# Counting channel work from the issue of a crossbar transpose, and writing the last output half in two pieces

One core of one Trainium2 chip (the other cores idle). The metric is the device time of one execution in microseconds; the time of a kernel is the median of its runs.

## The reference

Attention with squared ReLU, then an MLP mixer over tokens and channels: 8 batches, 12 heads, 448 tokens, head size 64, so 768 channels.

```python
scores = q @ k.T / sqrt(64);  attn = relu(scores)**2 / 448
x = (attn @ v), heads side by side                 # [8, 448, 768]
u = x + (relu(x.T @ w_tok1) @ w_tok2).T            # token product, 448 -> 256 -> 448
out = u + relu(u @ w_ch1) @ w_ch2                  # channel product, 768 -> 1536 -> 768
```

## The kernel before

Attention goes by "fours" of heads, 24 in all, in a loop of rounds. Round `i` makes the scores of four `i`, the values and the token products of four `i - 1`. The channel products of earlier batches lie in a queue as units (`channel1`: six matmuls of 448 columns; `channel2`: twelve of 384 columns, an add, and a store after each second one), and `fill` draws from it between the pieces of attention, so that TensorE always has something to do. The token product needs `x` with tokens on the partitions; from four 8 on that turn is a crossbar transpose by DMA (`x_back`), and what `fill` puts between the issue of the transpose and `token1_main` is what hides it.

```python
    def x_back(i, place="bank", copy=None):
        ...
        if i >= XDMA:                                   # XDMA = 8; round i + 1 issues it
            nc.sync.dma_start_transpose(
                out=x_sb.rearrange("n r c d -> n (r c) d"),
                in_=xT[b % 2][:, 2 * d : 2 * d + 2, :].rearrange("n r t -> n (r t)"),
            )
            return
        ...                                             # earlier: eight TensorE transposes and a copy

    def token1_main(i):
        ...                                             # six matmuls L294 that read x_sb

    C1 = 6 * 189
    C2 = 12 * 163

    def fill(share, least=0):
        if not queue:
            return
        credit[0] += share * rate[0]
        done = 0
        while queue and (credit[0] > 0 or done < least):
            cost, unit = queue.pop(0)
            credit[0] -= cost
            unit()
            done += 1

    for i in range(DB + 1, ND + 2):                     # rounds 4 to 25
        ...                                             # scores 0 and 1, values(i - 1), values_out, scores 2
        if i - 1 < XDMA:
            fill(1 / 3, least=1)
        if 0 <= i - 1 < ND:
            x_back(i - 1)                               # the issue
        ...                                             # u_back: transposes of u on the same queue; loads
        if i - 1 >= XDMA:
            fill(0.37, least=1)                         # "the first fill"
        ...                                             # scores 3 and 4, transposes of q and k
        if slow:                                        # rounds up to 6
            token1(i - 1)
            fill(1 / 3, least=1)
        else:
            fill(0.37, least=1)                         # "the second fill"
            if back:
                token1_main(i - 1)
        ...
```

In `channel2` the last half of the last tile is one block of 384 columns: twelve matmuls, one add, and two stores of 64 rows, one from SyncE's queue and one from ScalarE's.

## Time and profile before

| | before |
|---|---|
| median of its runs | 378.77 us (378.59 to 379.48, 4 runs; the prediction knew three of them) |
| span of the profiled execution | 375.9 us |
| TensorE busy | 364.3 us (97%) |
| TensorE's wait for a transpose (L294) | 1.0 us, one time |
| last matmul to the end | 4.2 us |

The busy share says only who the bound is. What a change of order can win is in the idle time of that engine, place by place; the lines are in the prediction below. A wait in the timeline stands in brackets after the row that waited: its length in us and what ended it.

### The profile page before, as it was taken

How to read it: one execution, taken by the hardware profiler on the slowest of the kernel's cores; microseconds unless marked ns; L12 is line 12 of the kernel's file. 1: busy time of each engine (PE TensorE's matmuls, PEld its weight loads, DVE VectorE, ACT ScalarE, POOL GpSimd, SP SyncE). 2: the span in 40 equal slices, each digit the busy share in tenths (PEclk: the TensorE clock that was granted, in tenths of full speed). 3: DMA queues.
4: the chain of work that ended last, by engine and by line, in shares of the span. 5: the costliest groups of instructions: out<-in, count | busy, mean ns of one | idle time of the engine just before them, and what ended most of it. 6: DMA issues, size and time to landing. Idle time of an engine off the chain costs nothing.

```text
span 375.9 us, 10212 instructions
## 1 busy us (share of the span) xinstructions
PE 364.3 (97%) x4367; PEld 200.6 (53%) x4367; DVE 212.8 (57%) x412; ACT 211.6 (56%) x313; POOL 100.7 (27%) x187
## 2 busy tenths in 40 slices
PE   7889999999999989999999999999999999999995
PEld 3544555555555545565555655555555654555563
DVE  2996688766568456475654685375555755131021
ACT  4987888776544357725775457752775456412400
POOL 8975448303130322330330304312210000000000
PEclk9999999999999999999999999999999999999999
DMA  8999999923999867656755577847550424233023
GB/s 152 122 148 201 172 206 178 179 44 68 138 158 213 169 101 115 89 99 158 99 96 91 112 146 132 129 58 158 111 94 13 103 76 99 56 70 85 0 64 105
DMA packets 69405, 43.32 MB, mean 115 GB/s; under 512 B 43440, under 2 KB 65904, under 8 KB 69360
## 3 DMA queue, kind: packets, MB, share of 16 engines
q0 software_dynamic: 24496, 21.49, 40.0%
q1 hardware_dynamic: 44560, 20.75, 25.6%
q8 instruction: 34, 0.56, 0.6%
q10 hardware_dynamic: 304, 0.43, 0.4%
q14 instruction: 11, 0.09, 0.1%
HBM read 43.42 MB, written 11.01 MB: 145 GB/s over the span
## 4 chain that ended last, share of the span: by engine, by line
PE 87%; DVE 6%; ACT 3%; DMA 2%; issue 1%; SPq 0%; ACTq 0%; DVEq 0%
PE m_ps L425 29%; PE m_ps L386 28%; PE acc_ps L205 9%; PE sc_ps L172 8%; PE h_ps L335 4%; PE t_ps L294 3%; PE qkT_ps L148 3%; DVE at L193 2%; ACT at L186 2%; DMA x_sb<-xT 1%; DVE uT_sb L345 1%; PE t_ps L310 1%; DMA k_first<-in_k_dram 1%; PE t_ps L276 1%; DVE qkT L162 1%; PE x_ps L258 1%
## 5 line engine op out<-in xcount | busy, mean ns | idle before, releaser
L186 ACT ACTIVATE at<-sc_ps 128x896 bf16<-128x896 f32 x167 | 144.9, 924 | 50.0 <-PE sc_ps L172 50.0
L193 DVE TENSOR_TENSOR at<-at 128x896 bf16<-128x896 bf16 x168 | 99.0, 625 | 52.2 <-ACT at L186 52.0
L386 PE MATMUL m_ps<-uT_sb,wc 128*128 128x448 bf16 x564 | 115.4, 353 | 0.2 <-DVE uT_sb L345 0.2
L425 PE MATMUL m_ps<-wc,r_sb 128*128 128x384 bf16 x672 | 115.3, 326 | 0.0
L425 PEld LDWEIGHTS <-r_sb 128*128 128x128 bf16 x672 | 63.8, 98 | 47.7 <-issue 6.4
L393 ACT ACTIVATE r_sb<-m_ps 128x448 bf16<-128x448 f32 x94 | 51.3, 546 | 56.4 <-PE m_ps L386 56.0
L386 PEld LDWEIGHTS <-wc 128*128 128x128 bf16 x564 | 52.4, 98 | 53.2 <-issue 7.9
L432 DVE TENSOR_TENSOR out_sb<-m_ps,u_sb 128x384 f32<-128x384 f32 x56 | 31.0, 553 | 48.3 <-PE m_ps L425 47.6
L172 PE MATMUL sc_ps<-qkT 64*64 64x448 bf16 x672 | 54.1, 358 | 1.0 <-ACT at L186 0.6
L205 PE MATMUL acc_ps<-at,v_raw 64*64 64x448 bf16 x672 | 41.0, 351 | 0.9 <-ACT x_sb L267 0.5
L223 DVE TENSOR_SCALAR xT<-acc_ps 128x448 bf16<-128x448 f32 x45 | 26.1, 619 | 27.6 <-PE acc_ps L205 27.6
L608 POOL COPY gate<-x_sb 1x1 bf16<-1x1 bf16 x12 | 2.7, 221 | 127.9 <-DMA x_sb<-xT 127.9
L84 POOL DMA_DIRECT2D q_raw<-in_q_dram x48 | 29.0, 616 | 19.6 <-DMA wc<-in_moe_w_ch_dram 16.7
L345 DVE TENSOR_TENSOR uT_sb<-h_ps,xT 128x448 bf16<-128x448 f32 x48 | 27.7, 615 | 10.5 <-PE h_ps L335 10.4
L84 POOL DMA_DIRECT2D v_raw<-in_v_dram x48 | 29.6, 645 | 6.0 <-DMA wc<-in_moe_w_ch_dram 4.4
L162 DVE COPY qkT<-qkT_ps 128x896 bf16<-128x896 bf16 x45 | 25.9, 615 | 9.2 <-PE qkT_ps L148 9.2
L320 ACT ACTIVATE r_sb<-t_ps 128x256 bf16<-128x256 f32 x36 | 11.8, 381 | 31.7 <-PE t_ps L310 27.6
L205 PEld LDWEIGHTS <-v_raw 64*64 64x64 bf16 x672 | 21.8, 106 | 14.6 <-issue 4.9
L172 PEld LDWEIGHTS <-qkT 64*64 64x64 bf16 x672 | 17.5, 105 | 21.6 <-issue 17.7
L84 POOL DMA_DIRECT2D k_raw<-in_k_dram x46 | 28.2, 637 | 1.7 <-issue 1.7
L335 PE MATMUL h_ps<-wt,r_sb 128*128 128x448 bf16 x96 | 22.3, 353 | 0.0
L294 PE MATMUL t_ps<-x_sb,wt 128*128 128x256 bf16 x108 | 14.7, 273 | 1.0 <-DMA x_sb<-xT 1.0
(50 smaller groups left out, 146.6 us busy)
## 6 DMA issues: line engine op xcount, KB each, us to landing
out_dram<-out_sb SPq DMA_DIRECT2D x54, 192.0 KB, 2.8
q_raw<-in_q_dram POOLq DMA_DIRECT2D x48, 112.0 KB, 4.2
v_raw<-in_v_dram POOLq DMA_DIRECT2D x48, 112.0 KB, 5.0
k_raw<-in_k_dram POOLq DMA_DIRECT2D x46, 112.0 KB, 4.8
wc<-in_moe_w_ch_dram POOLq DMA_DIRECT2D x4, 1152.0 KB, 10.6
u_sb<-uT_sb SPq DMA_TRANSPOSE x48, 2.6
x_sb<-xT SPq DMA_TRANSPOSE x16, 3.3
k_first<-in_k_dram SPq DMA_DIRECT2D x1, 224.0 KB, 3.7
```

The lines of the kernel that those rows point to most:

```text
L84: eng.dma_start(out=dst[64 * r : 64 * (r + 1)].rearrange("p g c d -> p g (c d)"), in_=src[b, h0 : h0 + 2].rearrange("g (p c) d -> p g (c d ...
L162: (nc.scalar.copy if split and r == 0 else nc.vector.tensor_copy)(sb[:, r].rearrange("n w t -> n (w t)"), parts[r][:, : 2 * S])
L172: nc.tensor.matmul(ps[64 * r : 64 * (r + 1), g, :S], lhsT=sb[h, r, 1, c * 64 : (c + 1) * 64], rhs=sb[h, r, 0, :], start=True, stop=True, s ...
L186: nc.scalar.activation(at, ps[:, :, :S], AF.Relu)
L193: nc.vector.tensor_tensor(out=at, in0=at, in1=at, op=ALU.mult)
L205: nc.tensor.matmul(ps[r][64 * g : 64 * (g + 1), :S], lhsT=v_raw[h, g, c, :], rhs=at[h, g, :], start=(c == 0), stop=(c == QC - 1), skip_gro ...
L335: nc.tensor.matmul(parts[r][:, :S], lhsT=r1[:, j, r * 128 : (r + 1) * 128], rhs=wt2[:, j, :], start=(j == 0), stop=(j == JC - 1),)
L345: nc.vector.tensor_tensor(out=uT_tiles[b // 2][:, 2 * d + r, off : off + S], in0=parts[r][:, :S], in1=xT[b % 2][:, 2 * d + r, :S], op=ALU.add,
L386: nc.tensor.matmul(ps[:, :S], lhsT=wc1[:, g, e * 128 : (e + 1) * 128], rhs=uT[:, g, off : off + S], start=(g == 0), stop=(g == CC - 1),)
L393: nc.scalar.activation(r2[:, e, off : off + S], ps[:, :S], AF.Relu)
L425: nc.tensor.matmul(ps[:, :HN], lhsT=r2[:, e, t * 128 : (t + 1) * 128], rhs=wc2[:, e, cols], start=(e == 0), stop=(e == EC - 1),)
L432: nc.vector.tensor_tensor(out=o[:, cols].rearrange("n (g d) -> n g d", d=128), in0=ps[:, :HN].rearrange("n (g d) -> n g d", d=128), in1=u_ ...
```

## The change

Its intent: the `credit` of `fill` is an average over rounds, so a round whose units happen to be small can leave too little work behind the transpose. The new floor `upto` counts what was emitted since the issue and goes on drawing until 4400 ns' worth stands ahead of `token1_main` (the costs `C1` and `C2` are in ns: matmuls of 448 columns start 189 ns apart in the trace, those of 384 columns 163 ns). The second part cuts the last output half into 256 and 128 columns, so that the add and the store that come after the last matmul are smaller.

```diff
--- before.py
+++ after.py
@@ -447,6 +447,33 @@
         if half == 1:
             out_tiles.pop((b, t))
 
+    def channel2_last(b, t):
+
+        r2, o = r2_tiles[b // 2], out_tiles[b, t]
+        cuts = (HN, HN + 256, DM)
+        for lo, hi in zip(cuts, cuts[1:]):
+            ps = ps_mm.tile([128, 512], FP32, tag="bank", name="m2_ps")
+            for e in range(EC):
+                nc.tensor.matmul(
+                    ps[:, : hi - lo],
+                    lhsT=r2[:, e, t * 128 : (t + 1) * 128],
+                    rhs=wc2[:, e, lo:hi],
+                    start=(e == 0),
+                    stop=(e == EC - 1),
+                )
+            nc.vector.tensor_tensor(
+                out=o[:, lo:hi].rearrange("n (g d) -> n g d", d=128),
+                in0=ps[:, : hi - lo].rearrange("n (g d) -> n g d", d=128),
+                in1=u_tiles[b][:, lo // 128 : hi // 128, t - chunks(b).start, :],
+                op=ALU.add,
+            )
+            for k in range(2):
+                n, c = divmod(2 * t + k, QC)
+                rows = out[2 * (b // 2) + n].rearrange("(p c) m -> c p m", c=QC)
+                (nc.scalar if k else nc.sync).dma_start(
+                    out=rows[c, :, lo:hi], in_=o[64 * k : 64 * (k + 1), lo:hi]
+                )
+
     queue, later = [], []
     C1 = 6 * 189
     C2 = 12 * 163
@@ -456,7 +483,10 @@
             queue.append((C1, lambda e=e: channel1(b, e)))
         for t in chunks(b):
             for j in range(2):
-                later.append((C2, lambda t=t, j=j: channel2(b, t, j)))
+                last = b == B - 1 and t == NT - 1 and j == 1
+                unit = channel2_last if last else channel2
+                args = (b, t) if last else (b, t, j)
+                later.append((C2, lambda unit=unit, args=args: unit(*args)))
         if b > 0:
             queue.extend(later)
             later.clear()
@@ -466,14 +496,17 @@
     credit = [0.0]
     rate = [EC * C1 / 3.5]
 
-    def fill(share, least=0):
+    since = [0.0]
+
+    def fill(share, least=0, upto=0):
         if not queue:
             return
         credit[0] += share * rate[0]
         done = 0
-        while queue and (credit[0] > 0 or done < least):
+        while queue and (credit[0] > 0 or done < least or since[0] < upto):
             cost, unit = queue.pop(0)
             credit[0] -= cost
+            since[0] += cost
             unit()
             done += 1
 
@@ -598,6 +631,7 @@
             fill(1 / 3, least=1)
         if 0 <= i - 1 < ND:
             x_back(i - 1)
+        since[0] = 0.0
         if i > 2 * DB + 1:
             if i == 2 * DB + 2:
                 hold_back(1, x_tiles[i - 1][:1, 0, 0, :1])
@@ -623,7 +657,7 @@
             token1(i - 1)
             fill(1 / 3, least=1)
         else:
-            fill(0.37, least=1)
+            fill(0.37, least=1, upto=4400 if back else 0)
             if back:
                 token1_main(i - 1)
         if i < ND:
```

## The prediction

> **What bounds the kernel now.** I read the page's busy line and slices first, then the list of who waited for whom (TensorE alone), then the timeline around the one wait that the change aims at, and last the end of the timeline.
>
> ```profile
> PE 364.3 (97%) x4367; PEld 200.6 (53%) x4367; DVE 212.8 (57%) x412; ACT 211.6 (56%) x313; POOL 100.7 (27%) x187
> PE   7889999999999989999999999999999999999995
> PEclk9999999999999999999999999999999999999999
> ```
>
> TensorE is the bound: 364.3 of 375.9 us, at full clock. So 11.6 us are all that can be won without taking work off TensorE. The windows of 10 us put them: 6.0 us in the first 40 us, 4.2 us after the last matmul, 1.0 us between 130 and 140 us, 0.2 to 0.3 us in two other windows. The list of TensorE's waits says what the middle one is:
>
> ```profile
> PE warm_ps L488 <- DVE warm L484: 1.2, 1, 1.2
> PE t_ps L294 <- DMA x_sb<-xT: 1.0, 1, 1.0
> PE qkT_ps L148 <- ACT k_raw L89: 0.9, 1, 0.9
> ```
>
> The columns are the total, how often, and the longest, in us. One single token product (L294) of 16 fed by a crossbar transpose waited for it, 1.0 us. The other long waits are of the start. Here is that place, round 11 of the main loop:
>
> ```profile
> 132.91 0.34 DVE L232 TENSOR_SCALAR xT<-acc_ps 128x64 bf16<-128x64 f32 x2
> 133.39 1.23 SPq L249 DMA_TRANSPOSE x_sb<-xT  x1
> 134.96 2.44 PE L386 MATMUL m_ps<-uT_sb,wc 128*128 128x448 bf16 x12
> 138.40 0.55 PEld L294 LDWEIGHTS <-wt 128*128 128x128 bf16 x6 [1.45 <-DMA x_sb<-xT]
> 138.41 0.83 PE L294 MATMUL t_ps<-x_sb,wt 128*128 128x256 bf16 x6 [1.01 <-DMA x_sb<-xT]
> ```
>
> The transpose is issued at 133.39; TensorE is through with its filler (two channel1 units) at 137.40 and then stands to 138.41. So its **lead** (issue to the earliest start of the token product) is 4.01 us and the landing took about 5.0. Round 14, where nothing waits, is the comparison that I lean on most:
>
> ```profile
> 178.56 1.25 SPq L249 DMA_TRANSPOSE x_sb<-xT  x1
> 179.31 3.58 PE L386 MATMUL m_ps<-uT_sb,wc 128*128 128x448 bf16 x18
> 182.59 0.18 POOL L608 COPY gate<-x_sb 1x1 bf16<-1x1 bf16 x1 [13.89 <-DMA x_sb<-xT]
> 182.73 0.82 PE L294 MATMUL t_ps<-x_sb,wt 128*128 128x256 bf16 x6
> ```
>
> Lead 182.73 - 178.56 = 4.17 us, and the gate copy shows the landing just before 182.59 (the trace has 182.47, 3.9 us after issue): 0.25 us to spare. The page's median landing is 3.3 us, so there must be a reason for 5.0.
>
> ```profile
> q8 instruction: 34, 0.56, 0.6%
> ```
>
> 34 packets of 16,384 bytes are instruction fetches. 0.56 MB over 2 x 4367 TensorE instructions is 64 bytes each, so I take this queue to be TensorE's. In the packet records one starts at 136.32 and takes 0.92 us, and from 136.4 on single 256-byte transposed rows take up to 1.57 us where they usually take 0.02. I put all the landings beside the fetches: with one starting 2.5 to 2.9 us after the issue the transpose took 5.4, about 5.0 and 4.7 us (issues at 103.14, 133.39, 207.09); 0.9 us after it, 3.9 us; just before, well before or well after it, 3.0 to 3.3 us, but for one of 4.05 (issue at 118.31) that fetches don't explain. So the 1.0 us is a short lead meeting a late fetch.
>
> The end:
>
> ```profile
> 363.74 7.96 PE L425 MATMUL m_ps<-wc,r_sb 128*128 128x384 bf16 x48
> 370.38 2.45 ACTq L444 DMA_DIRECT2D out_dram<-out_sb  x2
> 371.74 0.56 DVE L432 TENSOR_TENSOR out_sb<-m_ps,u_sb 128x384 f32<-128x384 f32 x1 [1.39 <-PE m_ps L425]
> ```
>
> The last matmul ends at 371.71, the add at 372.30, both queues issue at 372.32, packets run from about 373.45 to 374.35, and the program ends at 375.93.
>
> [...] The last store's 96 KB pieces landed 2.2 us after issue here, of which only some 0.9 us, for both queues together, is movement[...]. [...] This trace has 67 ns (eight 128-column transposes of L258 from 88.98 to the next matmul at 89.52), 163 ns at 384 (12 in 1.95 us) and 110 ns at 256 (six of L294 in 0.66).
>
> **The change, part by part.** I walked the queue of channel units by hand with its credits (channel1 counts 1134, channel2 1956), before and after.
>
> *The floor of 4400.* It counts what was emitted since the x_back of the round, and acts in the fill just ahead of the token product. No unit is added or dropped; units come forward. It bites in rounds 7 and 8 (one unit more each, where the transpose is still TensorE's own and nothing waits), 11, 17 and 23. Because rounds 7 and 8 have drawn ahead, round 11 is not what it was: before, it had one channel2 and two channel1 (1956+2268=4224, under the floor); after, the channel2 is already done and it has one channel1 and then three (4536). Round 12 loses units: from three plus three channel1 to one plus three. Rounds 17 and 23 just gain a channel1 of 1.14 us (6 x 0.19), taken from round 18 and 24.
>
> In time: the first of the two fills runs mostly before the issue, so round 11's lead rises not by 0.3 us but to that of the same arrangement in round 14: 4.17 instead of 4.01. That alone would win 0.16 of 1.0 us. What helps more is where the fetch falls. It hangs on a count of instructions: the one at 136.32 came in after the first channel1 behind the qk transposes, and after the change that point is passed at the same time, while the transpose is issued 1.95 us (one channel2) later, at about 135.3. The fetch is then 1.0 us after the issue, as in round 14 (0.9 us, landing 3.9). So I expect landing near 3.9 against a lead of 4.17: no wait, with little to spare. I count **0.75 us** of the 1.0, for a chance of about one in four that most of it stays. Round 12 (lead 4.17, fetch about 2 us before the issue, landing 3.3), 17 (lead 3.85 to 5.0) and 23 (3.44 to 4.6) wait neither before nor after; nothing is won there.
>
> *The last half in two.* TensorE: 12 x 110 + 12 x 67 = 2.12 us for 1.95, **+0.17**. [...] The last store moves 64 KB, not 192: of some 0.9 us of movement about 0.35 stays (an estimate[...]), **-0.55**. The first piece's two issues of 0.5 us each run on two queues from about 371.5 and are over when the second piece is ready at 372.2, and its 128 KB are on their way a us earlier. Sum **-0.6 us**. The rest of the end, landing to program end, stays.
>
> Together 0.75 + 0.6 = 1.35 us, less 0.05 for the rival below: 378.7 - 1.3 = **377.4 us**.
>
> **The rivals.** *The wait stays or moves.* For it: the lead is hardly longer and other landings took 5.4, 4.7 and 4.05 us; in round 12 the lead falls from 6.6 to 4.17. Against it: round 14. It would leave only the end's gain: 378.1, and with a second wait 378.7. *Round 9 begins to wait.* Two output tiles, not one, are now stored (768 KB in place of 384 KB) on the same SyncE queue between the u transposes, which fill it from 83.6 to 101.4, and the transpose at 103.14 (105.1 after). [...] its spare was 0.15 us. Against it: its fetch comes earlier too (1.6 in place of 2.9 us after the issue). It would cost 0.3 to 1 us; I give it one in five. *The end gains nothing*, if the second small store waits for the first piece's issue[...]: 377.9. *A full gain*, the 1.0 us gone and 0.8 at the end: 376.9. An engine that takes over as the bound I rule out: DVE and ACT are at 57% and their work only moves by a unit.
>
> **Range and chances.** The cases run from 376.9 to 378.7; the three runs of before span 0.9 us, so I widen below: 376.5 to 378.6. 2% is 7.6 us, more than all that TensorE idles in the middle and at the end together (5.5): within 2% 0.985, faster 0.01, slower 0.005.
>
> **What would show it.** Right: TensorE's list of waits has no L294 or one under 0.3 us; busy stays within 0.3 us of 364.3 (+0.17 for the split); the round-11 transpose is issued near 135.3, with a fetch about 1 us behind it; the last add is of 128 columns[...]; from the last matmul's end to the program's end 3.4 us in place of 4.2. Wrong: L294 waits near 110 us (round 9) or in rounds 11 and 12, or the end's stretch is unchanged.

The end came to -0.6 us from +0.17 (TensorE), -0.55 (the store) and a term for the smaller add; the whole was 0.75 + 0.6 less 0.05, so 1.3 us. The 3.4 us foretold from the last matmul to the end hold the term too. The traces give 553 ns for the add of 384 columns (before, L432) and 0.29 us for that of 128 (after, L464), so -0.26 for it. The 67, 163 and 110 ns are steps from the start of one matmul to the next, for 128, 384 and 256 columns. That the store's packets alone get shorter, and the 0.3 to 1 us of the round-9 rival, were estimates.

## The result

The changed kernel took **376.44 us** (376.01 to 377.34, 4 runs) against 378.77 us, ratio 0.9938 (95% interval 0.9915 to 0.9961): faster by 0.6%. A ratio here is the mean time of one kernel's runs over that of the other's of the same rounds, so not quite the ratio of the medians. Measured again with five rounds it was 376.79 us, ratio 0.9949. The prediction was 377.4 with a range of 376.5 to 378.6: direction right, the forecast gain too small, and the first measurement 0.06 us below the range.

The page after, TensorE's busy line:

```profile
PE 365.0 (98%) x4379; PEld 201.8 (54%) x4379; DVE 213.1 (57%) x413; ACT 211.5 (57%) x313; POOL 101.2 (27%) x187
```

The list of TensorE's waits after, its first rows (who waited for what: us in total, times, longest):

```profile
PE warm_ps L521 <- DVE warm L517: 1.2, 1, 1.2
PE warm_ps L528 <- DVE qkT L162: 0.7, 1, 0.7
PE sc_ps L172 <- ACT at L186: 0.6, 3, 0.2
```

L294 is gone from it; these rows are all of the start, and after 40 us the list has only two waits of 0.2 us. The timeline after at round 11, to be held against the one in the prediction:

```profile
133.93 1.31 PE L386 MATMUL m_ps<-uT_sb,wc 128*128 128x448 bf16 x6
135.41 1.25 SPq L249 DMA_TRANSPOSE x_sb<-xT  x1
136.15 3.58 PE L386 MATMUL m_ps<-uT_sb,wc 128*128 128x448 bf16 x18
139.57 0.82 PE L294 MATMUL t_ps<-x_sb,wt 128*128 128x256 bf16 x6
139.59 0.18 POOL L642 COPY gate<-x_sb 1x1 bf16<-1x1 bf16 x1 [11.60 <-DMA x_sb<-xT]
```

One channel1 ahead of the issue and three behind it, as the queue said: lead 139.57 - 135.41 = 4.16 us. The transpose landed after 4.06 us, 0.1 us before it was needed. That is a narrow escape, not a margin.

The end in the timeline after:

```profile
368.43 2.14 PE L457 MATMUL m_ps<-wc,r_sb 128*128 128x256 bf16 x24
369.94 0.42 DVE L464 TENSOR_TENSOR out_sb<-m_ps,u_sb 128x256 f32<-128x256 f32 x1 [0.75 <-PE m_ps L457]
370.39 1.39 ACTq L473 DMA_DIRECT2D out_dram<-out_sb  x2
370.61 0.29 DVE L464 TENSOR_TENSOR out_sb<-m_ps,u_sb 128x128 f32<-128x128 f32 x1 [0.25 <-PE m_ps L457]
```

(Rows of one kind are merged, so L457 shows the form of its first matmul only.) The last matmul ends at 370.57 and the program at 374.24: 3.67 us where it was 4.23.

**Where the time went.** The two profiles differ by 375.93 - 374.24 = 1.69 us. The wait explains 1.17 of it: more than the 1.01 us of idle time that the row shows, because where nothing waits L294 starts some 0.17 us before the modelled end of the matmul ahead (its drain; 0.16 us at each of the 18 such places of after), and that overlap is lost too. I took "the wait in full" from the distance between the starts of the L294 matmul and of the one ahead of it, less the usual distance of such a pair. The end explains 0.56. Together 1.73.

### The profile page after: what moved, and what is told of

Same layout as the page of the kernel before. It is cut to its first block, busy times and chain, and to the rows that moved or that the text cites. A ratio compares the mean times of both kernels' runs of the same rounds, so it can differ in the third digit from the quotient of the medians.

```text
span 374.2 us, 10241 instructions
## 1 busy us (share of the span) xinstructions
PE 365.0 (98%) x4379; PEld 201.8 (54%) x4379; DVE 213.1 (57%) x413; ACT 211.5 (57%) x313; POOL 101.2 (27%) x187
## 4 chain that ended last, share of the span: by engine, by line
PE 90%; DVE 5%; ACT 3%; issue 1%; DVEq 0%; ACTq 0%
PE m_ps L425 29%; PE m_ps L386 28%; PE sc_ps L172 9%; PE acc_ps L205 9%; PE h_ps L335 4%; PE t_ps L294 3%; PE qkT_ps L148 3%; ACT at L186 2%; DVE at L193 2%; PE t_ps L310 1%; DVE uT_sb L345 1%; PE t_ps L276 1%; PE warm_ps L521 1%; DVE qkT L162 1%; PE x_ps L258 1%
## 5 line engine op out<-in xcount | busy, mean ns | idle before, releaser
L425 PE MATMUL m_ps<-wc,r_sb 128*128 128x384 bf16 x660 | 113.2, 326 | 0.0
L425 PEld LDWEIGHTS <-r_sb 128*128 128x128 bf16 x660 | 62.7, 98 | 46.7 <-issue 6.1
L432 DVE TENSOR_TENSOR out_sb<-m_ps,u_sb 128x384 f32<-128x384 f32 x55 | 30.6, 556 | 48.3 <-PE m_ps L425 46.8
L294 PE MATMUL t_ps<-x_sb,wt 128*128 128x256 bf16 x108 | 14.7, 273 | 0.0
```

What stands on the lines that cost most here:

```text
L425: nc.tensor.matmul(ps[:, :HN], lhsT=r2[:, e, t * 128 : (t + 1) * 128], rhs=wc2[:, e, cols], start=(e == 0), stop=(e == EC - 1),)
L432: nc.vector.tensor_tensor(out=o[:, cols].rearrange("n (g d) -> n g d", d=128), in0=ps[:, :HN].rearrange("n (g d) -> n g d", d=128), in1=u_ ...
```

## Experiments

Twelve kernels ran. The theory at the outset: one short lead and a slow end, each measured by its row in the profile. What was open: why the timed gain (2.3 us) exceeded the profiles' (1.7 us), and whether the fetch or something else makes a landing late.

### 1 to 4: noise, each half alone, the whole again

**before_again**, no edit:

> The kernel before, unchanged, for a second profile and for the noise. The profiled execution of before took 377.7 us, its timed ones 378.6 to 379.5, so about 1 us is in the timed runs that the profile does not show. Theory A (the profile fell on a lucky execution, other executions of before wait more for crossbar transposes): times spread over about 1 us, and this profile, if it is slower than 375.9 us, shows more than 1.0 us of waits of the token product L294. Theory B (the profile is typical, and the extra is the start or the end): the L294 waits are again 1.0 us in one place, and whatever else differs sits before 40 us or after the last matmul. Ratio to before 1.000 within 0.002 in both.

**floor_only**: `last = b == B - 1 and ...` becomes `last = False`.

> The floor of 4400 alone, the last half in one piece as before. In the profile 1.2 us less than before (the 1.0 us that TensorE stood plus some 0.17 us, the modelled drain of the matmul ahead of the wait, which overlaps the next one when nothing waits); the last matmul to the end 4.2 us as before. Theory A: 1.7 us or so less in the timed runs, ratio 0.9955. Theory B: 1.2 us less, ratio 0.997.

**split_only**: `upto=4400 if back else 0` becomes `upto=0`.

> The last half in two pieces alone, the units in the order of before. Last matmul to the end 3.7 us in place of 4.2; the L294 wait in round 11 stays, 1.0 us. Both theories: 0.5 us less, ratio 0.9986, and floor and split add up to the whole change.

**after_again**, no edit to the changed kernel:

> The changed kernel, unchanged, on the same chip as the two halves. Ratio 0.994 again within 0.002 if theory A holds; 0.9955 (1.7 us, the difference of the two profiles) if the first measurement was partly noise. The profile again without a wait of L294 over 0.3 us.

| kernel | median us | ratio to before | 95% interval | waits for the transpose in its profile, in full | last matmul to end |
|---|---|---|---|---|---|
| before_again | 378.12 | 0.9994 | 0.9971 to 1.0018 | 1.65 us (rounds 10, 11) | 4.22 us |
| floor_only | 377.21 | 0.9965 | 0.9947 to 0.9983 | 0 | 4.22 us |
| split_only | 378.12 | 0.9988 | 0.9969 to 1.0007 | 1.57 us (rounds 9, 11, some in 14) | 3.65 us |
| after_again | 376.79 | 0.9949 | 0.9930 to 0.9968 | 0.82 us (rounds 11, 14) | 3.65 us |

The halves add up: 0.9965 x 0.9988 = 0.9953 against 0.9949. The floor is worth about 1.3 us and the split about 0.5. The split's interval just includes 1, so its verdict rests on the profiles, where the end takes 4.22 to 4.23 us in every kernel with the last half in one piece, and 3.61 to 3.67 us in every one with the two pieces and their two stores.

The second profile of before shows a second wait:

```profile
PE t_ps L294 <- DMA x_sb<-xT: 1.3, 2, 1.0
```

So theory A is half right: the first profile of before was a lucky execution, others wait in round 9 or 10 too. And the changed kernel is not free of waits either: its second profile has 0.26 us in round 11 and 0.23 us in round 14. Theory B is half right too: the rest of the scatter is the start. The first channel1 matmul stands at 33.3 and 33.4 us in the first two profiles and between 33.1 and 34.9 us in the others, whichever the kernel. A count that leaves the start out agrees with the gain of the floor: from that matmul to the end of the last one it is 338.4, 338.9 and 338.8 us in the three profiles with the old order (before, before_again, split_only) and 337.2, 337.2 and 338.1 us in floor_only, after and after_again. Theory A's 1.7 us for the floor alone was not seen (1.3; the interval from 0.6 to 2.0 doesn't exclude it).

### 5 and 6: moving the instruction fetches

The edit, to before (**before_shift140**) and to the changed kernel (**after_shift140**), in the warm-up at the start:

```diff
+    for m in range(70):
+        hr = slice(64 * (m % 2), 64 * (m % 2) + 64)
+        nc.tensor.matmul(warm_ps[hr, :64], lhsT=warm[hr, :64], rhs=warm[hr, :64],
+                         start=True, stop=True, skip_group_check=True)
```

> The kernel before with 70 tiny matmuls (140 TensorE instructions) more at the start, while TensorE waits for k anyway: nothing else changes, but every later instruction fetch falls 140 instructions earlier. Theory F (a wait is a late fetch beside a transpose whose lead is short): the fetch of round 11 comes 0.6 us after the issue in place of 2.9, so it lands within 4.0 us and its 1.0 us wait is gone; fetches now fall 2.1 us after the issue of round 17 (lead 3.85) and 1.7 us after that of round 23 (lead 3.44), which land in 4.3 us or more, so new waits of 0.4 to 1.0 us each appear there. Rival G (round 11 is slow for the stores and loads around it, fetches are a coincidence): the wait in round 11 stays at 1.0 us and rounds 17 and 23 do not wait. Time, F and G: within 0.3% of before.

> The changed kernel with the same 140 instructions more at the start. Theory F: the leads of rounds 17 and 23 are 5.0 and 4.6 us here, so the fetches that fall there (about 2.1 and 1.7 us after the issue) cost nothing, no wait over 0.3 us: the floor is worth 2 us or so against the shifted kernel before, if that one waits twice. Rival G: as the changed kernel, no waits either, but then the difference to the shifted kernel before is 1.2 us plus 0.5 for the end.

Timelines of before_shift140, round 11 and then round 17:

```profile
134.81 1.23 SPq L249 DMA_TRANSPOSE x_sb<-xT  x1
138.66 0.82 PE L294 MATMUL t_ps<-x_sb,wt 128*128 128x256 bf16 x6
...
223.16 1.23 SPq L249 DMA_TRANSPOSE x_sb<-xT  x1
227.96 0.83 PE L294 MATMUL t_ps<-x_sb,wt 128*128 128x256 bf16 x6 [0.80 <-DMA x_sb<-xT]
```

The wait of round 11, there in both profiles of before and in split_only, is gone; a new one stands in round 17 (and one of 0.60 us in round 14). Beside the fetches (packets of 16,384 bytes in the trace's packet records, 0.88 to 1.70 us each in before; times after the issue of the transpose):

| kernel | round | fetch starts | landing | idle of L294 |
|---|---|---|---|---|
| before | 11 | +2.9 us | about 5.0 us | 1.01 us |
| before_shift140 | 11 | -1.1 us | 3.27 us | none |
| before | 17 | -1.1 us | not recorded | none |
| before_shift140 | 17 | +2.5 us | 4.76 us | 0.80 us |
| before | 14 | +0.9 us | 3.91 us | none |
| before_shift140 | 14 | +2.6 us | 4.88 us | 0.60 us |
| after | 11 | +1.1 us | 4.06 us | none |
| after_shift140 | 12 | +2.8 us | 4.83 us | 0.38 us |
| after_shift140 | 14 | +2.7 us | not recorded | 0.65 us |
| after_shift140 | 17 | +2.4 us | 4.78 us | none (lead 5.0) |

All fourteen profiles together say the same. Of the transposes with a recorded landing, 36 had a fetch that started 2.2 to 3.0 us after the issue, and every one of them landed late, after 4.4 to 5.5 us (median 4.84). In 128 no fetch started between issue and landing, and they landed after 3.0 to 4.1 us (median 3.25).

Theory F holds in what it is about: the waits go where the fetches go, and rival G is out, since round 11 has the same stores and loads around it and lands in 3.27 us. My forecast of the places was only half right: I expected rounds 17 and 23 and got 14 and 17. A fetch follows a count of TensorE's instructions, but loosely: the number of them started ahead of the n-th of the 34 fetches differs between the traces of before and after by at most 10 for 27 fetches and by 17 to 128 for the other seven, so it can't be planned to a microsecond.

The miss that matters: I expected the floor to be worth 2 us under the shift. By the profiles it was worth nothing there. after_shift140 waits in rounds 9, 12 and 14, in full 2.16 us, against 2.00 us for before_shift140; from the first channel1 matmul to the end of the last one it takes 339.5 us against 339.2. The ratios to before are 1.0025 (1.0008 to 1.0041) and 1.0035 (1.0022 to 1.0049), and their difference is about what the split brings. These ratios are a little unfair to after_shift140: its times exceed the spans by 1.8 to 3.0 us, where the excess is 1.7 to 1.9 us in every other kernel but late_5600_shift140 (1.8 to 2.2), and no trace shows what the rest is. By the spans, means of six executions, it is 0.9 us under before_shift140; less the split's 0.5, that leaves some 0.4 us for the floor, within the scatter and far from 2. Round 17, where the floor had made the lead 5.0 us, did not wait; rounds 12 and 14, where the floor is content with a lead of 4.2 to 4.3 us, did. In round 9 the order that the floor makes took lead away: the input of the transpose was ready at 105.43 us, but SyncE's queue was issuing four output stores until 105.98 and came to it at 106.08. So **most of the floor's 1.3 us in the kernel as it stands depends on where the fetches happen to fall**.

### 7 and 8: the floor in one round, and a higher floor

**floor_11_only**: no split, and `upto=5000 if i == 11 else 0`.

> The kernel before with the floor in round 11 alone (no drawing ahead in rounds 7 and 8, none in 17 and 23, the last half in one piece). One channel2 and three channel1 stand behind the issue, lead 4.0 + 1.14 = 5.15 us; the fetch stays 2.9 us after the issue and the landing at 5.0 us. Expected: no wait of L294 in round 11 (or under 0.2 us), 1.2 us less than before, ratio 0.997: the whole of what the floor alone brought. Rival: rounds 7 and 8 bring a part by their other order, then 0.5 us or less.

377.91 us, ratio 0.9980 (0.9968 to 0.9993). In the profile round 11 did not stand: lead 4.99 us, landing 4.94, the fetch at +2.7. Round 14 waited 0.19 us this time (landing 4.47). Lead alone is thus enough to end the round-11 wait, though with only 0.05 us to spare. The gain, 0.8 us (the interval runs from 0.3 to 1.2), lies between the two expectations (1.2, and 0.5 or less), and the round-14 wait, 0.36 us in full, makes up the greater part of what is missing to 1.2.

**floor_5000**: `upto=5000 if back else 0`, with the split.

> The whole change with the floor at 5000 instead of 4400. In rounds 11, 14, 17, 20 and 23 one channel1 and four more stand behind the transposes, lead 5.3 us or so in place of 4.2. If what is left in the changed kernel is the odd wait of 0.2 to 0.5 us in rounds 11 and 14 (the second profile of it had 0.26 and 0.23), 0.3 us less than the changed kernel and no L294 wait at all, ratio to before 0.994. If drawing ahead starves a later round, slower than the changed kernel.

377.26 us, ratio 0.9966 (0.9951 to 0.9982): no better than 4400 (0.9949; the intervals overlap, so the times alone don't show it worse). All L294 waits are gone, and a new one came at 102 us:

```profile
101.47 0.56 DVE L432 TENSOR_TENSOR out_sb<-m_ps,u_sb 128x384 f32<-128x384 f32 x1 [6.12 <-DMA u_sb<-uT_sb]
102.09 2.11 PE L425 MATMUL m_ps<-wc,r_sb 128*128 128x384 bf16 x12 [1.46 <-DVE out_sb L432]
```

In rounds 7 and 8 the higher floor draws output units so far ahead that their adds need `u` before the twelve transposes of `u` on SyncE's queue have brought it. VectorE sits for 6.12 us, the two tiles `m_ps` that hold the sums of the channel units stay taken, and TensorE waits 1.46 us for one. With 4400 the same kind of wait of VectorE is there, 1.47 us in after and 3.33 us in after_shift140, but it doesn't reach TensorE. In rounds 7 and 8 the floor has nothing to hide anyway, as `x` is turned by TensorE there.

### 9 and 10: a higher floor where it is needed

**late_5600**: `upto=5600 if back and i > 2 * DB + 2 else 0`, with the split; that is, from round 9 on. **late_5600_shift140**: the same with the 70 matmuls.

> The changed kernel with the floor at 5600 and only from round 9 on; rounds 7 and 8 keep the order of before, so the output adds of round 8 do not come ahead of the u transposes. Leads by the queue: at least 5.0 us in each of rounds 9 to 24. Theory F (waits are late fetches beside a short lead): no L294 wait anywhere and no wait of L425 for its add near 102 us; profile 0.3 to 0.6 us under the two profiles of the changed kernel less their starts; ratio to before 0.993 to 0.995. Rival H (drawing ahead always shifts a wait to the adds): a wait of L425 of over 0.5 us somewhere, no gain over the changed kernel.

> The same with the 140 TensorE instructions at the start. The changed kernel with these had waits of 0.58, 0.38 and 0.65 us in rounds 9, 12 and 14 where fetches came 2.7 to 3.3 us after the issue. Theory F: fetches come at such places again but the leads of rounds 12 and 14 are 5.3 us or more, so none of those waits stays; round 9 (lead 5.5) waits 0.2 us at most. About 2 us (three waits and 0.17 us of drain each) less than the changed kernel so shifted: ratio to before 0.997 where that had 1.0025. Rival: 1.0025 again, the 140 instructions themselves cost the time.

**late_5600** took 375.61 us (375.41 to 375.84), ratio 0.9916 (0.9896 to 0.9935), the fastest of all. Its list of TensorE's waits:

```profile
PE warm_ps L521 <- DVE warm L517: 1.2, 1, 1.2
PE warm_ps L528 <- DVE qkT L162: 0.7, 1, 0.7
PE sc_ps L172 <- ACT at L186: 0.6, 3, 0.2
```

In round 11 the fetch comes at +2.9 us and the landing takes 4.97 us, as in before, but the lead is 6.1 us. The reason for late landings is still there, and it costs nothing. Under the shift it keeps its gain: 376.71 us, ratio 0.9947 (0.9928 to 0.9966), against 1.0025 for after_shift140 and 1.0035 for before_shift140 (by the spans, each against before, 2.4 us under after_shift140). In that profile round 12 landed in 4.83 us as it did there, and did not wait. What remains is 0.27 us of idle time in round 10 (landing 5.85 us) and 0.06 us in round 9. Compared with late_5600 it is still 0.3% slower; these two waits are 0.65 us in full, and its first channel1 matmul stands at 34.9 us where that of late_5600 stands at 33.5. That the 140 instructions cost something of their own is thus not excluded. Theory F expected 0.993 to 0.995, and 0.997 under the shift; rival H expected no gain over the changed kernel. Measured were 0.9916, whose interval just reaches F's 0.993, and 0.9947, clear of F's 0.997. One lead was not what the queue promised: 4.27 us in round 24, where the landing took 3.23.

That surplus is not settled. late_5600's profile is 0.53 us under that of the changed kernel though neither waits in L294. The starts of the matmuls after 40 us show that about 0.3 us each came from those of the values and those of the scores standing closer together. Why another order of units does that I did not test.

### 11 and 12: the end

**three_pieces**: `cuts = (HN, HN + 128, HN + 256, DM)`.

> The changed kernel with its last half in three pieces of 128 columns. The last add and the last store are as in two pieces; TensorE needs 12 x 0.06 us more or less the same. If the end is set by the last piece alone: last matmul to the end 3.7 us as with two pieces, no gain. If the store of the first piece stood in the way of the last one's: 0.2 us less. If six issues on two queues stand in each other's way (0.5 us each): the last issue comes later and the end grows by 0.2 to 0.5 us.

**one_store**: two pieces of matmuls and adds, one store of 384 columns.

```diff
-            for k in range(2):
+            for k in range(2 if hi == DM else 0):
...
-                    out=rows[c, :, lo:hi], in_=o[64 * k : 64 * (k + 1), lo:hi]
+                    out=rows[c, :, HN:], in_=o[64 * k : 64 * (k + 1), HN:]
```

> The changed kernel with two pieces of matmuls and adds but one store of all 384 columns after the second add: the add's share of the end's gain without the store's. Last matmul to issue 0.35 us as in the changed kernel (0.61 before), issue to end 3.6 us as before (3.25 in the changed kernel): from the last matmul to the end 3.95 us, half-way between 4.2 and 3.7. If the small store brings nothing: 3.7.

The end of one_store, then of three_pieces, in their timelines:

```profile
371.18 0.29 DVE L464 TENSOR_TENSOR out_sb<-m_ps,u_sb 128x128 f32<-128x128 f32 x1 [0.24 <-PE m_ps L457]
371.50 0.50 ACTq L473 DMA_DIRECT2D out_dram<-out_sb  x1
```

```profile
368.60 2.31 PE L457 MATMUL m_ps<-wc,r_sb 128*128 128x128 bf16 x36
370.02 2.09 ACTq L473 DMA_DIRECT2D out_dram<-out_sb  x3
370.94 0.29 DVE L464 TENSOR_TENSOR out_sb<-m_ps,u_sb 128x128 f32<-128x128 f32 x1 [0.38 <-PE m_ps L457]
```

| kernel | last matmul to last issue | last issue to end | sum |
|---|---|---|---|
| before | 0.63 us | 3.60 us | 4.23 us |
| one_store | 0.36 us | 3.59 us | 3.95 us |
| three_pieces | 0.65 us | 3.29 us | 3.94 us |
| after | 0.42 us | 3.26 us | 3.67 us |

one_store came out as expected, 3.95 us: half of the end's gain is the smaller add, half the smaller store. (Its time, 377.09 us and 0.9956, carries the floor too.) three_pieces loses 0.27 us of the gain, as its third expectation said: ScalarE's queue is still at its second issue when the last add is done at 371.23, and its last issue comes only at 371.56. Of the three ways tried, the two pieces with two stores give the shortest end. The time of three_pieces, 376.77 us and 0.9949, can't tell it from the changed kernel.

## Why the prediction was right or wrong

- **Where time could be won** (one L294 wait and the end): right. No other stretch of the profile changed by more than the scatter of the start. One of the signs failed: TensorE's busy time rose by 0.7 us and not by 0.3 at most. The first 10 us, where neither part of the change acts, rose by 0.9 (7.57 to 8.45).
- **The walk of the queue and the round-11 arrangement**: right, but for one reading. Issue at 135.41 (135.3 foretold), lead 4.16 (4.17), fetch 1.1 us after the issue (1.0), landing 4.06 (3.9), no wait. But the lead of 4.01 us that it read for round 11 before runs to the modelled end of the matmul ahead, while the 4.17 of round 14 runs to the start of L294. On one footing round 11 had 3.85 us, as the same arrangement of units has in round 17, so the change added 0.31 us of lead and not 0.16.
- **The term of 0.75 us for the floor**: this is the step that failed, in size and not in kind. Measured, it was about 1.3 us. First, the idle time in the row (1.0) left out the 0.17 us of drain that a wait costs too: 1.17 was there to be won. Second, I took a quarter off for the chance that the wait stays; in the first profile none of it stayed, in the second 0.82 us of waits in rounds 11 and 14 did. Third, I read one execution of before as every execution: its second profile had 1.65 us and split_only's had 1.57. Over the three profiles with the old order the waits average 1.46 us, over the five with the floor at 4400 and no shift (floor_only, after, after_again, one_store, three_pieces with 0, 0, 0.82, 0 and 0.35) 0.23 us: 1.2 us won. The first measurement's 2.3 us still exceeds this and the end by 0.5 us; that did not repeat, and I take it for the scatter of executions.
- **The end, -0.6 us**: the sum was right (0.56 measured), its terms were not. TensorE pays 0.02 us and not 0.17, mainly because its 128-column matmuls start 56 ns apart and not 67. The 67 was a misreading: the 0.54 us of the eight transposes are seven steps of 56 ns and one of 150 ns to the matmul of another kind that follows. The add gives 0.26 us (0.55 to 0.29), but 0.05 us of that is lost again before ScalarE's queue issues. The store gives 0.34 and not 0.55: its packets carry a third of the bytes, but run for 0.60 us (372.15 to 372.76 in after) where they ran for 0.92 (373.44 to 374.36 in before).
- **Rivals.** "Round 9 begins to wait" was wrong in the kernel as it stands (landing 4.59 us, 0.96 us to spare) and right under the shift (0.58 us, landing 5.66, against 0.04 us in before_shift140), where the stores on SyncE's queue that it named held the issue back. "The wait stays or moves" happens from execution to execution: the rounds with little to spare, 11 and 14, are those that waited in the second profile. That this rival is the normal state for other places of the fetches is what I had not seen.
- **The range**: 1.2 + 0.56 is 1.8 us, which gives 376.9, inside it. The first measurement, 2.3 us, was on the far side, the second, 1.9 us by its ratio, is not. The low bound should have had the whole wait in full, the end and the scatter of the start, about 376.

## What to carry to other kernels

Compare the lead behind each asynchronous transfer with its worst landing in several profiles, not with its median: here 3.2 us was usual, and in the fourteen profiles every landing over 4.1 us, up to 5.9, had an instruction fetch that started between issue and landing. A floor tuned to the kernel's present layout can win by luck; shift the layout by a few dummy instructions and see whether the gain stays. And when work is drawn forward to hide one wait, look at what that work itself waits for: the floor helped from round 9 on and, at 5000, hurt in rounds 7 and 8.
